# A new order for the end of a weight stream, another pitch for keys and values, and a last product written as four rows

## The chip, the cores and the metric

The kernel runs on one core of a Trainium2 chip. The metric is device time in microseconds (us), the median of several runs. A run's time is some 1.8 us above the span that the profile shows (370.68 against 368.9 in the profiled run of the kernel before); traces are told here in microseconds from the start of the span. The record has the span of every run, profiled or not. Every run told here was in the fast state.

The engines are called PE (matrix products), PEld (its weight loads), DVE (vector), ACT (activations), POOL and SP (which issues the large loads).

Ratios are the mean time of one kernel's fast runs over the mean of the other's fast runs of the same rounds, so they are not quite the ratio of the medians quoted beside them. Intervals are 95%.

## The reference

One token passes through a transformer block with adaptive layer norm. It attends with 32 query heads to 8 key/value heads of 32768 cached keys of 128 elements each, then goes through a small feed-forward layer. Cut to what matters:

```python
mod = (_silu(c) @ w_mod).reshape(c.shape[0], 6, 1, -1)       # sa, ca, ga, sb, cb, gb
h = _layernorm(x) * (1 + ca) + sa
q = h @ wq                                                   # 512 -> 32 heads x 128
o = softmax(q @ k_cache.T * Dh ** -0.5) @ v_cache            # 2 x 64 MB of keys and values
x = x + ga * (o @ wo)                                        # 4096 -> 512, 4 MB
h = _layernorm(x) * (1 + cb) + sb
x = x + gb * (relu(h @ w1) @ w2)                             # 512 -> 1792 -> 512, 1.8 + 1.8 MB
```

## The kernel before

All large inputs come through one queue of loads, issued in a fixed order into a ring of eight slots of 2 MB; a load is issued when the slot that it takes is free. Keys and values of one head group g come in four tiles (u = 0..3) of 2 MB, and the keys run one group ahead of the values.

```python
TK = 64
kv = A_k_cache[0].rearrange("g (u p j) d -> g u p j d", p=P, j=TK)   # one tile: 2 MB in one piece
vv = A_v_cache[0].rearrange("g (u p j) d -> g u p j d", p=P, j=TK)
w2_v = B_w2.rearrange("(p ft) d -> p ft d", p=P)
ring = ctx.enter_context(tc.tile_pool(name="ring", bufs=8))
ktpool = ctx.enter_context(tc.tile_pool(name="ktpool", bufs=4))
...
stream = [("wm", 0), ("wm", 1), ("wq", 0), ("wq", 1)]
stream += [("k", 0, u) for u in range(NTILE)]
for g in range(Hkv):
    for u in range(NTILE):
        if g + 1 < Hkv:
            stream.append(("k", g + 1, u))
        stream.append(("v", g, u))
    if g % GH == GH - 2:
        stream.append(("wo", g // GH))
stream += [("w1",), ("w2a",), ("w2b",)]
...
for g in range(Hkv):
    for u in range(NTILE):
        if g + 1 < Hkv:
            scores(g + 1, u)      # DVE transposes the keys, PE multiplies
        pv(g, u)                  # 16 products of 512 columns on PE
    if g + 1 < Hkv:
        softmax(g + 1)
    gather(g)
    if g % GH == GH - 1:
        project(g // GH)          # normalise, then 64 products with wo
```

So wo's second half is streamed between the values of group 6 and those of group 7, the last group. The tail computes in columns (512 values as 128 partitions x 4), and the output goes out as 128 pieces of four elements:

```python
w1_f = w1_sb[:].rearrange("p kt (m ft) -> p kt ft m", ft=FT)      # weights read with a step of 14
...
for part, base, n in (("w2a", 0, FT - W2B), ("w2b", FT - W2B, W2B)):
    for f in range(n):
        for ko in range(KT):
            nc.tensor.matmul(ffnT_ps[:, ko:ko + 1],               # 128 weights, one column
                lhsT=w2_sb[:, f, :].rearrange("p (m ko) -> p ko m", ko=KT)[:, ko, :],
                rhs=hidT[:, base + f:base + f + 1], ...)
...
nc.scalar.dma_start(out=out[0, 0].rearrange("(p kt) -> p kt", p=P), in_=outT_bf[:])
```

Of the kernel before, what the change touches and what calls it, by code (L numbers as in the profile page):

```python
# [9 lines left out]
BF16 = mybir.dt.bfloat16  # L10
# [7 lines left out]
def kernel(  # L18
# [29 lines left out]
    CH = P // HH  # L48
    RH = Dh // CH
    NHALF = Hkv // GH  # L50
    W2B = 2
    assert Dh == 128 and REP == 4 and D == 512 and Dff % P == 0 and NTILE == 4
    scale = float(Dh) ** -0.5
    eps = 1e-5


    kv = A_k_cache[0].rearrange("g (u p j) d -> g u p j d", p=P, j=TK)
    vv = A_v_cache[0].rearrange("g (u p j) d -> g u p j d", p=P, j=TK)
    wm_v = w_mod.rearrange("(p kt) n -> p kt n", p=P)
    wq_v = A_wq.rearrange("(p kt) n -> p kt n", p=P)  # L60
    wo_v = A_wo.rearrange("(b p r) d -> b p r d", p=P, r=RH)
    w1_v = B_w1.rearrange("(p kt) f -> p kt f", p=P)
    w2_v = B_w2.rearrange("(p ft) d -> p ft d", p=P)

    const = ctx.enter_context(tc.tile_pool(name="const", bufs=1))
    ring = ctx.enter_context(tc.tile_pool(name="ring", bufs=8))
    ktpool = ctx.enter_context(tc.tile_pool(name="ktpool", bufs=4))
    spool = ctx.enter_context(tc.tile_pool(name="spool", bufs=2))
    ps_s = ctx.enter_context(tc.tile_pool(name="ps_s", bufs=2, space=bass.MemoryType.PSUM))
    ps_o = ctx.enter_context(tc.tile_pool(name="ps_o", bufs=2, space=bass.MemoryType.PSUM))  # L70
# [9 lines left out]
    def load(key):  # L80
        kind = key[0]
        if kind == "wm":
            t = ring.tile([P, KT // 2, 6 * D], BF16, tag="slot", name="wm_sb")
            src = wm_v[:, 2 * key[1]:2 * key[1] + 2, :]
        elif kind == "wq":
            t = ring.tile([P, KT // 2, Hq * Dh], BF16, tag="slot", name="wq_sb")
            src = wq_v[:, 2 * key[1]:2 * key[1] + 2, :]
        elif kind == "k":
            t = ring.tile([P, TK, Dh], BF16, tag="slot", name="Ksb")
            src = kv[key[1], key[2]]  # L90
        elif kind == "v":
            t = ring.tile([P, TK, Dh], BF16, tag="slot", name="Vsb")
            src = vv[key[1], key[2]]
        elif kind == "wo":
            t = ring.tile([P, RH, D], BF16, tag="slot", name="wo_sb")
            src = wo_v[key[1]]
        elif kind == "w1":
            t = ring.tile([P, KT, Dff], BF16, tag="slot", name="w1_sb")
            src = w1_v
        elif kind == "w2a":  # L100
            t = ring.tile([P, FT - W2B, D], BF16, tag="slot", name="w2a_sb")
            src = w2_v[:, 0:FT - W2B, :]
        else:
            t = ring.tile([P, W2B, D], BF16, tag="slot", name="w2b_sb")
            src = w2_v[:, FT - W2B:FT, :]
        i = nc.sync.dma_start(out=t[:], in_=src)
        tc.stamp_issue_order_token(i.ins, "sp_stream")
        loaded[key] = t
# [3 lines left out]
    for g in range(Hkv):  # L112
        for u in range(NTILE):
            if g + 1 < Hkv:
                stream.append(("k", g + 1, u))
            stream.append(("v", g, u))
        if g % GH == GH - 2:
            stream.append(("wo", g // GH))
    stream += [("w1",), ("w2a",), ("w2b",)]
    pos = [0]  # L120

    def need(key):
        while key not in loaded:
            load(stream[pos[0]])
            pos[0] += 1
        return loaded[key]
# [106 lines left out]
                )  # L233
    modT_sb = const.tile([P, NMOD], F32)
    nc.vector.tensor_copy(out=modT_sb[:], in_=modT_ps[:])

    hT = const.tile([P, KT], BF16)
    layernorm_T(xT[:], hT[:], modT_sb[:, 0:KT], modT_sb[:, KT:2 * KT], "ln1")
# [128 lines left out]
                start=False, stop=(gl == GH - 1 and s == 3), skip_group_check=True,  # L367
            )

    def project(b):  # L370

        oh_ps = acc.pop(b)
        linv = spool.tile([HH, 1], F32, tag="linv", name="linv")
        nc.vector.reciprocal(out=linv[:], in_=oh_ps[:, Dh:Dh + 1])  # L374
        oh = spool.tile([HH, Dh], BF16, tag="oh_sb", name="oh_sb")
        nc.vector.tensor_scalar(
            out=oh[:], in0=oh_ps[:, 0:Dh], scalar1=linv[:], scalar2=None, op0=ALU.mult,
        )
        o2_ps = small_ps([P, RH], "o2_ps")
        for cc in range(CH):  # L380
            nc.tensor.matmul(  # L381
                o2_ps[:], lhsT=esel[:, cc, :, :].rearrange("h x y -> h (x y)"),
                rhs=oh[:, RH * cc:RH * (cc + 1)], start=(cc == 0), stop=(cc == CH - 1),
            )
        o2 = spool.tile([P, RH], BF16, tag="o2_sb", name="o2_sb")
        nc.vector.tensor_copy(out=o2[:], in_=o2_ps[:])
        wo_sb = need(("wo", b))
        for r in range(RH):
            for ko in range(KT):
                nc.tensor.matmul(  # L390
                    attnT_ps[:, ko:ko + 1],
                    lhsT=wo_sb[:, r, :].rearrange("p (m ko) -> p ko m", ko=KT)[:, ko, :],
                    rhs=o2[:, r:r + 1], start=False, stop=(b == NHALF - 1 and r == RH - 1),
                    skip_group_check=True,
                )
# [5 lines left out]
    for g in range(Hkv):  # L401
        if g + 1 < Hkv:
            build_qbd(g + 1)
        for u in range(NTILE):
            if g + 1 < Hkv:
                scores(g + 1, u)
            pv(g, u)
        PT_tiles.pop(g)
        if g + 1 < Hkv:
            softmax(g + 1)  # L410
        gather(g)
        if g % GH == GH - 1:
            project(g // GH)


    x1T = const.tile([P, KT], F32)
# [2 lines left out]
    h2T = const.tile([P, KT], BF16)  # L419
    layernorm_T(x1T[:], h2T[:], modT_sb[:, 3 * KT:4 * KT], modT_sb[:, 4 * KT:5 * KT], "ln2")  # L420

    w1_sb = need(("w1",))
    w1_f = w1_sb[:].rearrange("p kt (m ft) -> p kt ft m", ft=FT)
    hidT_ps = small_ps([P, FT], "hidT_ps")
    for ft in range(FT):
        for kt in range(KT):
            nc.tensor.matmul(  # L427
                hidT_ps[:, ft:ft + 1], lhsT=w1_f[:, kt, ft, :], rhs=h2T[:, kt:kt + 1],
                start=(kt == 0), stop=(kt == KT - 1),
            )  # L430
    hidT = const.tile([P, FT], BF16)
    nc.scalar.activation(out=hidT[:], in_=hidT_ps[:], func=ACT.Relu)
    ffnT_ps = small_ps([P, KT], "ffnT_ps")
    nc.vector.memset(ffnT_ps[:], 0.0)
    for part, base, n in (("w2a", 0, FT - W2B), ("w2b", FT - W2B, W2B)):
        w2_sb = need((part,))
        for f in range(n):
            for ko in range(KT):
                nc.tensor.matmul(  # L439
                    ffnT_ps[:, ko:ko + 1],  # L440
                    lhsT=w2_sb[:, f, :].rearrange("p (m ko) -> p ko m", ko=KT)[:, ko, :],
                    rhs=hidT[:, base + f:base + f + 1], start=False, stop=(base + f == FT - 1),
                    skip_group_check=True,
                )
    oT_f = const.tile([P, KT], F32)
    nc.vector.tensor_tensor(out=oT_f[:], in0=ffnT_ps[:], in1=modT_sb[:, 5 * KT:6 * KT], op=ALU.mult)
    outT_bf = const.tile([P, KT], BF16)
    nc.vector.tensor_tensor(out=outT_bf[:], in0=oT_f[:], in1=x1T[:], op=ALU.add)
    nc.scalar.dma_start(out=out[0, 0].rearrange("(p kt) -> p kt", p=P), in_=outT_bf[:])


# [28 lines left out]
```

## Time and profile before

| | before |
|---|---|
| time, median of 3 runs | 370.83 us (370.71 to 370.88) |
| span of the profiled execution | 368.9 us |
| bytes read, rate while the stream runs | 149.4 MB, 423 to 432 GB/s |
| last V tile landed | 346.84 us |
| first product with wo's second half | 353.44 us |
| output issued | 365.06 us |

From the page, the busy time of each engine (us, share of the span, instructions):

```profile
PE 287.7 (78%) x1616; PEld 124.1 (34%) x1616; DVE 179.2 (49%) x189; ACT 31.6 (9%) x73; POOL 9.4 (3%) x15
```

No compute engine is near 100%, while the transfers (shown in the prediction) are at one rate all the way to the tail. One more stretch of the timeline also belongs here later: the 64 products of the last group's V (start us, us, engine, line, operation, output and inputs, count, and in brackets the idle time before it and what ended it).

```profile
332.20 8.58 PE L353 MATMUL o_ps<-Vsb,PT_g 128*16 128x512 bf16 x32 [0.71 <-DMA Vsb<-in_A_v_cache_dram]
341.99 3.61 PE L353 MATMUL o_ps<-Vsb,PT_g 128*16 128x512 bf16 x16 [1.21 <-DMA Vsb<-in_A_v_cache_dram]
346.88 3.61 PE L353 MATMUL o_ps<-Vsb,PT_g 128*16 128x512 bf16 x16 [1.28 <-DMA Vsb<-in_A_v_cache_dram]
```

PE waits for each of the last tiles: it has caught up with the stream. The transfer of wo's second half, which comes just before these tiles, gave it the time. It even had time for a slow stretch: the first 32 products take 8.58 us, where two tiles at the pace of the last ones take 7.2, and PE still waits 1.21 us for the next tile. The granted clock (the share of full speed that PE is allowed) is low there; the last three values of a stretch are this clock, the DMA share and GB/s, after the busy time of PE, PEld, DVE, ACT and POOL:

```profile
330.00:335.00 5.00, 3.98 (x17) 1.74 (x18) 1.25 (x1) 0.27 (x2) 0.00 (x0) 0.69 0.99 423
```

Read in stretches of 0.5 us, it is 0.50 from 331.9 to 335.3 us.

### The profile page before, as it was taken

The numbers are of one execution on the slowest core, as the hardware profiler recorded it, in microseconds if no ns is written. First come the engines' busy times: TensorE is split into PE (matmuls) and PEld (weight loads), VectorE is DVE, ScalarE is ACT, GpSimd is POOL, SyncE is SP. The second block draws the span as 40 slices with busy tenths as digits, with TensorE's granted clock in tenths as the row PEclk, the third lists the DMA queues.
The fourth block names the chain that finished last, engine by engine and source line by source line (L and its number), as shares of the span: only waits on it lengthen the run. The fifth ranks groups of instructions, "written<-read, shape, count | busy, mean of one in ns | idle before, by whom it ended". The sixth has DMA issues, their size and how long they took to land.

```text
span 368.9 us, 3738 instructions
## 1 busy us (share of the span) xinstructions
PE 287.7 (78%) x1616; PEld 124.1 (34%) x1616; DVE 179.2 (49%) x189; ACT 31.6 (9%) x73; POOL 9.4 (3%) x15
## 2 busy tenths in 40 slices
PE   0448867987977798796878899987968799779755
PEld 0433322333322333232323343333323333233344
DVE  1419966556554464436454473546445645420020
ACT  1111031003000300012000300011000200020020
POOL 9000000000000000000000000000000000000000
PEclk9999998998999989986999979999989789998975
DMA  8999999999999999999999999999999999999920
GB/s 303 428 428 425 428 427 432 428 430 426 423 430 428 426 428 426 428 428 426 426 429 430 428 424 423 428 432 432 426 428 426 426 426 426 425 428 426 426 110 0
DMA packets 10960, 149.66 MB, mean 406 GB/s; under 512 B 1600, under 2 KB 1600, under 8 KB 1728
## 3 DMA queue, kind: packets, MB, share of 16 engines
q1 hardware_dynamic: 10512, 149.43, 95.6%
q8 instruction: 12, 0.20, 0.2%
q10 hardware_dynamic: 432, 0.00, 0.1%
q14 instruction: 4, 0.03, 0.0%
HBM read 149.42 MB, written 0.00 MB: 405 GB/s over the span
## 4 chain that ended last, share of the span: by engine, by line
DMA 75%; PE 11%; DVE 11%; ACT 1%; issue 1%; DVEq 0%
DMA Ksb<-in_A_k_cache_dram 64%; DVE KTt L287 10%; DMA Vsb<-in_A_v_cache_dram 9%; PE o_ps L353 4%; PE S_ps L296 4%; DMA xc_bf<-in_c_dram 2%; PE attnT_ps L390 1%; PE hidT_ps L427 1%; PE ffnT_ps L439 1%; PE oh_ps L365 0%; DVE S_g L302 0%; ACT P_g L329 0%; DVE PT_g L334 0%; ACT X L363 0%; PE o_ps L381 0%
## 5 line engine op out<-in xcount | busy, mean ns | idle before, releaser
L287 DVE STREAM_TRANSPOSE KTt<-Ksb 128x2048 f32<-128x2048 f32 x64 | 144.4, 2287 | 67.7 <-DMA Ksb<-in_A_k_cache_dram 67.7
L296 PE MATMUL S_ps<-KTt,qbd 128*128 128x512 bf16 x512 | 136.3, 416 | 34.3 <-DVE KTt L287 33.3
L353 PE MATMUL o_ps<-Vsb,PT_g 128*16 128x512 bf16 x512 | 119.7, 389 | 4.2 <-DMA Vsb<-in_A_v_cache_dram 3.2
L296 PEld LDWEIGHTS <-qbd 128*128 128x128 bf16 x512 | 51.4, 102 | 114.1 <-issue 70.2
L353 PEld LDWEIGHTS <-PT_g 128*16 128x16 bf16 x512 | 44.5, 91 | 77.0 <-issue 21.2
L302 DVE TENSOR_SCALAR_CACHE_REDUCE S_g<-S_ps 128x512 f32<-128x512 f32 x16 | 11.0, 688 | 38.7 <-PE S_ps L296 38.7
L266 ACT COPY qbd<-qrep_sb 32x128 bf16<-32x128 bf16 x32 | 9.4, 295 | 183.5 <-PE S_ps L296 182.4
L363 ACT COPY X<-o_ps 16x512 f32<-16x512 f32 x8 | 4.6, 574 | 106.3 <-PE o_ps L353 106.3
L334 DVE STREAM_TRANSPOSE PT_g<-P_g 128x1024 bf16<-128x1024 bf16 x8 | 9.7, 1218 | 7.4 <-ACT P_g L329 7.3
L230 PE MATMUL modT_ps<-siluT,wm_sb 128*128 128x1 bf16 x96 | 3.5, 172 | 12.4 <-DVE siluT L222 12.4
L314 DVE TENSOR_REDUCE Mrow<-mT_ps 1x4 f32<-1x128 f32 x8 | 2.2, 279 | 20.6 <-PE mT_ps L312 20.6
L365 PE MATMUL oh_ps<-X,osel 16*16 16x128 f32 x64 | 10.6, 313 | 1.1 <-ACT X L363 1.1
L340 PE MATMUL oh_ps<-l_g,lsel 128*16 128x1 f32 x16 | 1.6, 171 | 11.4 <-ACT P_g L329 11.4
L374 DVE RECIPROCAL linv<-oh_ps 16x1 f32<-16x1 f32 x2 | 0.3, 135 | 20.7 <-PE oh_ps L365 20.7
L329 ACT ACTIVATE P_g<-S_g,nbias 128x1024 bf16<-128x1024 f32 x8 | 9.2, 1148 | 0.4 <-ACT nbias L326 0.2
L244 PE MATMUL qT_ps<-hT,wq_sb 128*128 128x1 bf16 x128 | 3.7, 165 | 5.7 <-DMA wq_sb<-in_A_wq_dram 5.1
L230 PEld LDWEIGHTS <-wm_sb 128*128 128x128 bf16 x96 | 3.6, 119 | 12.3 <-DMA wm_sb<-in_w_mod_dram 7.1
L365 PEld LDWEIGHTS oh_ps<-X,osel 16*16 16x16 f32 x64 | 6.0, 103 | 3.5 <-ACT X L363 1.8
L324 PE MATMUL Mb_ps<-ident_f,Mexp 1*128 1x1 f32 x16 | 3.0, 256 | 3.7 <-DVE Mexp L319 3.7
L244 PEld LDWEIGHTS <-wq_sb 128*128 128x128 bf16 x128 | 3.6, 104 | 5.9 <-DMA wq_sb<-in_A_wq_dram 5.2
L340 PEld LDWEIGHTS oh_ps<-l_g,lsel 128*16 128x16 f32 x16 | 0.9, 97 | 12.6 <-ACT P_g L329 9.7
L427 PE MATMUL hidT_ps<-h2T,w_sb 128*128 128x1 bf16 x56 | 3.5, 198 | 1.7 <-DVE h2T L213 1.7
(79 smaller groups left out, 60.7 us busy)
## 6 DMA issues: line engine op xcount, KB each, us to landing
Ksb<-in_A_k_cache_dram SPq DMA_DIRECT2D x32, 2048.0 KB, 33.6
Vsb<-in_A_v_cache_dram SPq DMA_DIRECT2D x32, 2048.0 KB, 33.7
wq_sb<-in_A_wq_dram SPq DMA_DIRECT2D x2, 2048.0 KB, 17.1
wo_sb<-in_A_wo_dram SPq DMA_DIRECT2D x2, 2048.0 KB, 32.6
wm_sb<-in_w_mod_dram SPq DMA_DIRECT2D x2, 1536.0 KB, 8.1
w_sb<-in_B_w_dram SPq DMA_DIRECT2D x1, 1792.0 KB, 33.3
w2a_sb<-in_B_w_dram SPq DMA_DIRECT2D x1, 1536.0 KB, 32.7
w2b_sb<-in_B_w_dram SPq DMA_DIRECT2D x1, 256.0 KB, 27.9
```

Source lines behind the costliest of these rows:

```text
L230: nc.tensor.matmul(modT_ps[:, j * KT + ko:j * KT + ko + 1], lhsT=lhsT[:, ko, :], rhs=siluT[:, kt:kt + 1], start=(kt == 0), stop=(kt == KT ...
L244: nc.tensor.matmul(qT_ps[:, hq:hq + 1], lhsT=wq_sb[kt // 2][:, kt % 2, hq * Dh:(hq + 1) * Dh], rhs=hT[:, kt:kt + 1], start=(kt == 0), stop ...
L266: nc.scalar.copy(out=o, in_=i)
L287: nc.vector.transpose(out=KTt[:].bitcast(F32), in_=Ksb[:, 32 * half:32 * half + 32, :].rearrange("p j d -> p (j d)").bitcast(F32),)
L296: nc.tensor.matmul(S_ps[:], lhsT=qbd[g % 2][:, hp, s, :], rhs=KTv[:, 16 * sl:16 * sl + 16, h, :, par], start=(t4 == 0 and sl == 0 and hp = ...
L302: nc.vector.tensor_scalar(out=S_tiles[g][:, G, :], in0=S_ps[:], scalar1=1.0, scalar2=None, op0=ALU.mult, op1=ALU.max, accum_out=m_tiles[g] ...
L329: nc.scalar.activation(out=P_g[:], in_=S_g[:].rearrange("p g f -> p (g f)"), func=ACT.Exp, bias=nbias[:], scale=scale, accum_out=l_g[:],)
L334: nc.vector.transpose(out=PT_g[:], in_=P_g[:])
L353: nc.tensor.matmul(o_ps[:], lhsT=PT_g[:, c0:c0 + 16], rhs=Vsb[:].rearrange("p (s j) d -> p s j d", j=16)[:, :, j, :], start=(u == 0 and j ...
L363: nc.scalar.copy(out=X[:], in_=o_tiles.pop(g)[:])
L365: nc.tensor.matmul(acc[b][:, 0:Dh], lhsT=osel[:, gl, s, :], rhs=X[:, s * Dh:(s + 1) * Dh], start=False, stop=(gl == GH - 1 and s == 3), sk ...
L427: nc.tensor.matmul(hidT_ps[:, ft:ft + 1], lhsT=w1_f[:, kt, ft, :], rhs=h2T[:, kt:kt + 1], start=(kt == 0), stop=(kt == KT - 1),)
```

## The change

The intent is to shorten the tail. Both halves of wo move behind all values, so that the long chain from the last V tile (product, gather, normalise) runs while wo, w1 and w2 still stream. The rest is to make the tail itself cheaper. The core of the diff:

```diff
-    kv = A_k_cache[0].rearrange("g (u p j) d -> g u p j d", p=P, j=TK)
-    vv = A_v_cache[0].rearrange("g (u p j) d -> g u p j d", p=P, j=TK)
+    kv = A_k_cache[0].rearrange("g (p u j) d -> g u p j d", p=P, j=TK)
+    vv = A_v_cache[0].rearrange("g (p u j) d -> g u p j d", p=P, j=TK)
-    w2_v = B_w2.rearrange("(p ft) d -> p ft d", p=P)
+    w2_v = B_w2.rearrange("(a p b) d -> p a b d", p=P, b=FB)           # FB = 2
-    ktpool = ... bufs=4
+    ktpool = ... bufs=3
-        if g % GH == GH - 2:
-            stream.append(("wo", g // GH))
+    stream += [("wo", b) for b in range(NHALF)]
     stream += [("w1",), ("w2a",), ("w2b",)]
+    def rows4(src_T, name):                   # a column vector as four rows
+        r_ps = small_ps([P, P], f"{name}_ps")
+        nc.vector.memset(r_ps[:], 0.0)
+        for i in range(KT):
+            dst = r_ps[32 * i:32 * i + 1, :].rearrange("o (n kt) -> o kt n", kt=KT)
+            for kt in range(KT):
+                nc.tensor.matmul(dst[:, kt, :], lhsT=src_T[:, kt:kt + 1],
+                                 rhs=ident_f[:, 32 * i:32 * i + 32], start=True, stop=True, ...)
+        nc.vector.tensor_copy(out=r_sb[:], in_=r_ps[:])
+    gb_rows = rows4(modT_sb[:, 5 * KT:6 * KT], "gb_rows")
...
         if g % GH == GH - 1:
-            project(g // GH)
+            normalise(g // GH)
+    for b in range(NHALF):
+        project(b)
...
+    x1_rows = rows4(x1T[:], "x1_rows")
-    w1_f = w1_sb[:].rearrange("p kt (m ft) -> p kt ft m", ft=FT)
+    w1_f = w1_sb[:].rearrange("p kt (a m b) -> p kt a b m", m=P, b=FB)    # step of 2
...
+                for i in range(KT):                                        # four column tiles
+                    nc.tensor.matmul(ffn_ps[32 * i:32 * i + 1, :], lhsT=hidT[:, ft:ft + 1],
+                        rhs=w2_sb[:, a, b, i * P:(i + 1) * P], ...)
...
-    nc.scalar.dma_start(out=out[0, 0].rearrange("(p kt) -> p kt", p=P), in_=outT_bf[:])
+    nc.sync.dma_start(out=out[0, 0].rearrange("(i n) -> i n", i=KT),
+        in_=o_bf[:].rearrange("(i r) n -> i r n", r=32)[:, 0, :])
```

More of the change, by code (lines that the diff above doesn't have):

```diff
@@ L50 @@
     NHALF = Hkv // GH
-    W2B = 2
-    assert Dh == 128 and REP == 4 and D == 512 and Dff % P == 0 and NTILE == 4
+    FB = 2
+    FA = FT // FB
+    assert Dh == 128 and REP == 4 and D == 512 and Dff % (FB * P) == 0 and NTILE == 4
     scale = float(Dh) ** -0.5
     eps = 1e-5
-    kv = A_k_cache[0].rearrange("g (u p j) d -> g u p j d", p=P, j=TK)
-    vv = A_v_cache[0].rearrange("g (u p j) d -> g u p j d", p=P, j=TK)
+    kv = A_k_cache[0].rearrange("g (p u j) d -> g u p j d", p=P, j=TK)
+    vv = A_v_cache[0].rearrange("g (p u j) d -> g u p j d", p=P, j=TK)
     wm_v = w_mod.rearrange("(p kt) n -> p kt n", p=P)
@@ L62 @@
     w1_v = B_w1.rearrange("(p kt) f -> p kt f", p=P)
-    w2_v = B_w2.rearrange("(p ft) d -> p ft d", p=P)
+    w2_v = B_w2.rearrange("(a p b) d -> p a b d", p=P, b=FB)
     const = ctx.enter_context(tc.tile_pool(name="const", bufs=1))
     ring = ctx.enter_context(tc.tile_pool(name="ring", bufs=8))
-    ktpool = ctx.enter_context(tc.tile_pool(name="ktpool", bufs=4))
+    ktpool = ctx.enter_context(tc.tile_pool(name="ktpool", bufs=3))
     spool = ctx.enter_context(tc.tile_pool(name="spool", bufs=2))
@@ L100, in load @@
         elif kind == "w2a":
-            t = ring.tile([P, FT - W2B, D], BF16, tag="slot", name="w2a_sb")
-            src = w2_v[:, 0:FT - W2B, :]
-        else:
-            t = ring.tile([P, W2B, D], BF16, tag="slot", name="w2b_sb")
-            src = w2_v[:, FT - W2B:FT, :]
+            t = ring.tile([P, FA - 1, FB, D], BF16, tag="slot", name="w2a_sb")
+            src = w2_v[:, 0:FA - 1]
+        else:
+            t = ring.tile([P, 1, FB, D], BF16, tag="slot", name="w2b_sb")
+            src = w2_v[:, FA - 1:FA]
         i = nc.sync.dma_start(out=t[:], in_=src)
@@ L235 @@
     nc.vector.tensor_copy(out=modT_sb[:], in_=modT_ps[:])
+    def rows4(src_T, name):
[4 more added lines that the diff above has]
+            for kt in range(KT):
+                nc.tensor.matmul(
+                    dst[:, kt, :], lhsT=src_T[:, kt:kt + 1], rhs=ident_f[:, 32 * i:32 * i + 32],
+                    start=True, stop=True, skip_group_check=True,
+                )
+        r_sb = const.tile([P, P], F32, name=f"{name}_sb")
+        nc.vector.tensor_copy(out=r_sb[:], in_=r_ps[:])
+        return r_sb
+    gb_rows = rows4(modT_sb[:, 5 * KT:6 * KT], "gb_rows")
     hT = const.tile([P, KT], BF16)
@@ L368, in gather, with normalise @@
             )
-    def project(b):
+    o2_tiles = {}
+    def normalise(b):
         oh_ps = acc.pop(b)
@@ L386, in project @@
         nc.vector.tensor_copy(out=o2[:], in_=o2_ps[:])
+        o2_tiles[b] = o2
+    def project(b):
+        o2 = o2_tiles.pop(b)
         wo_sb = need(("wo", b))
@@ L427 @@
             nc.tensor.matmul(
-                hidT_ps[:, ft:ft + 1], lhsT=w1_f[:, kt, ft, :], rhs=h2T[:, kt:kt + 1],
+                hidT_ps[:, ft:ft + 1], lhsT=w1_f[:, kt, ft // FB, ft % FB, :], rhs=h2T[:, kt:kt + 1],
                 start=(kt == 0), stop=(kt == KT - 1),
@@ L432 @@
     nc.scalar.activation(out=hidT[:], in_=hidT_ps[:], func=ACT.Relu)
-    ffnT_ps = small_ps([P, KT], "ffnT_ps")
-    nc.vector.memset(ffnT_ps[:], 0.0)
-    for part, base, n in (("w2a", 0, FT - W2B), ("w2b", FT - W2B, W2B)):
+    ffn_ps = small_ps([P, P], "ffn_ps")
+    nc.vector.memset(ffn_ps[:], 0.0)
+    for part, base, n in (("w2a", 0, FA - 1), ("w2b", FA - 1, 1)):
         w2_sb = need((part,))
-        for f in range(n):
-            for ko in range(KT):
-                nc.tensor.matmul(
-                    ffnT_ps[:, ko:ko + 1],
-                    lhsT=w2_sb[:, f, :].rearrange("p (m ko) -> p ko m", ko=KT)[:, ko, :],
-                    rhs=hidT[:, base + f:base + f + 1], start=False, stop=(base + f == FT - 1),
-                    skip_group_check=True,
-                )
-    oT_f = const.tile([P, KT], F32)
-    nc.vector.tensor_tensor(out=oT_f[:], in0=ffnT_ps[:], in1=modT_sb[:, 5 * KT:6 * KT], op=ALU.mult)
-    outT_bf = const.tile([P, KT], BF16)
-    nc.vector.tensor_tensor(out=outT_bf[:], in0=oT_f[:], in1=x1T[:], op=ALU.add)
-    nc.scalar.dma_start(out=out[0, 0].rearrange("(p kt) -> p kt", p=P), in_=outT_bf[:])
+        for a in range(n):
+            for b in range(FB):
+                ft = (base + a) * FB + b
+                for i in range(KT):
+                    nc.tensor.matmul(
+                        ffn_ps[32 * i:32 * i + 1, :], lhsT=hidT[:, ft:ft + 1],
+                        rhs=w2_sb[:, a, b, i * P:(i + 1) * P], start=False, stop=(ft == FT - 1),
+                        skip_group_check=True,
+                    )
+    o_rows = const.tile([P, P], F32)
+    nc.vector.tensor_tensor(out=o_rows[:], in0=ffn_ps[:], in1=gb_rows[:], op=ALU.mult)
+    o_bf = const.tile([P, P], BF16)
+    nc.vector.tensor_tensor(out=o_bf[:], in0=o_rows[:], in1=x1_rows[:], op=ALU.add)
+    nc.sync.dma_start(
+        out=out[0, 0].rearrange("(i n) -> i n", i=KT),
+        in_=o_bf[:].rearrange("(i r) n -> i r n", r=32)[:, 0, :],
+    )
 _INS = ['A_x', 'A_k_cache', 'A_v_cache', 'A_wq', 'A_wo', 'B_x', 'B_w1', 'B_w2', 'c', 'w_mod']
```

## The prediction

> **What bounds the kernel now.** I read the page's slices first, then the transfer issues, the chain of waits, the stretches of the last 25 us, and the timeline of the tail.
>
> The slices (40 slices of 9.22 us; tenths busy, then GB/s):
>
> ```profile
> DMA  8999999999999999999999999999999999999920
> GB/s 303 428 428 425 428 427 432 428 430 426 423 430 428 426 428 426 428 428 426 426 429 430 428 424 423 428 432 432 426 428 426 426 426 426 425 428 426 426 110 0
> ```
>
> The 16 DMA engines never starve: 423 to 432 GB/s for some 345 us, then nothing. So the span has two parts: a stream of 149.4 MB whose rate is set by the engines, and a tail in which nothing moves. Compute is not the bound in the first part (PE is busy 78% and DVE 49% of the span). Work taken from the middle is worth nothing; the time changes only through the rate of the stream or through the tail.
>
> The tail, from the chain that ended last (start us, us, what):
>
> ```profile
> 312.30 34.54 DMA Vsb<-in_A_v_cache_dram
> 346.84 0.04 issue
> 346.88 3.63 PE o_ps L353 x16
> ...
> 353.44 2.27 PE attnT_ps L390 x64
> 355.74 0.17 DVE x1T L417
> ...
> 358.89 3.48 PE hidT_ps L427 x56
> 362.40 0.19 ACT hidT L432
> 362.59 0.04 issue
> 362.63 2.01 PE ffnT_ps L439 x56
> 364.67 0.17 DVE oT_f L446
> 364.86 0.16 DVE outT_bf L448
> ```
>
> The last V tile lands at 346.84, and everything after it is serial: its product, the gather and normalisation up to 353.44, the wo product, layer norm, w1, w2, output. Only w1, w2a and w2b (3.58 MB) stream meanwhile. From the issue lines, start plus time to landing puts them at 317.80 + 33.3 = 351.1, 322.11 + 32.7 = 354.8 and 327.62 + 27.9 = 355.5 us: each has landed before the chain wants it (358.9, 362.6 and 364.2). Thus the end follows from the landing of the last V tile, 22 us before it.
>
> The output transfer and the stretch behind (issue line: times to landing, last column):
>
> ```profile
> wo_sb<-in_A_wo_dram SPq DMA_DIRECT2D x2, 2048.0 KB, 32.6
> out_dram<-outT_bf ACTq DMA_DIRECT2D x1, 1.0 KB, 2.8
> ```
>
> It is issued at 365.06, lands at 367.86, and the span ends 1.04 us later at 368.9. The timed median is 370.83.
>
> [...] The keys and values go from a 16 KB pitch (one contiguous 2 MB block per tile) to 64 KB[...]. The trace has one case between: wq's tiles are 16 KB pieces 32 KB apart, and they land within the stretch from 12 to 22 us, which ran at 431 GB/s against 427 for 27 to 346 us. [...] No four-tile product is in this trace. [...] granted clock 1.00 up to 355 us, 0.50 from 356 on.
>
> **The change part by part.**
>
> *Stream order.* Both wo tiles (2 MB each) move behind all V. Total bytes and the 3.58 MB at the end stay, so wo's second half takes exactly the place of the last V tile: if the rate holds, it lands at 346.84. The last V tile lands 2 x 4.9 = 9.8 us earlier, near 337.0; with its product, gather and normalisation (346.84 to 353.44, 6.6 us) it is done by 343.6, the first wo product (2.3 us) by 345.9, all under the wo stream. The instruction order agrees: both normalisations and the first 64 wo products precede the second's wait. So the chain starts with a 2.27 us product at 346.9 rather than with the V product: saved 353.44 - 346.88 = 6.56 us.
>
> *Rows for the residual.* x1 is turned into four rows by 16 fp32 products of 1 x 32, listed between the statistics product and w1 on PE. On DVE the copy of their result stands ahead of the layer norm's reciprocal in program order[...], so the layer norm must wait for them. Each fp32 product is two instructions in this trace; eight with 128 columns took 1.06 us at full clock (0.13 each). With 32 columns at half clock I take 0.055 each: 32 x 0.055 = 1.75 us, plus some 0.25 for the result and 0.3 for the copy of 128x128. The reciprocal came 357.95 - 356.56 = 1.39 us after the start of the statistics product; now it comes 0.58 + 1.75 + 0.25 + 0.3 = 2.9 us after. Cost: 1.5 us. The same 16 products for the gate run at 16 us, under the stream, where wq's second half was awaited until 22.1: free.
>
> *w1 product.* Its weights were read with a step of 14 elements; 56 products took 3.48 us, 62 ns each. The wo and w2 products, with a step of 4, took 2.27/64 = 35 and 2.01/56 = 36 ns, the latter at half clock. The new split of w1 makes the step 2. I take 34 ns: 1.9 us. Saved: 1.55 us.
>
> *w2 product.* 56 products, now a one-column weight with 128 moving columns, in four column tiles. The last V tile's 16 products of 512 columns took 3.63 us at full clock, 0.227 each, so 128 columns take 57 ns, or some 113 at half clock. If four run side by side that is 28 ns each; issue at some 36 ns, as above, is the floor. I take 2.3 us for 2.01. Cost: 0.3 us.
>
> *End.* Two DVE operations on 128x128 instead of 128x4: 0.16 us each becomes about 0.24 (a cast of 128x128 from PSUM took 0.29). Cost: 0.15 us. The output goes as four pieces of 256 B rather than 128 of 8 B; I guess 2.3 us for 2.8. Saved: 0.5 us.
>
> *Sum.* -6.56 + 1.5 - 1.55 + 0.3 + 0.15 - 0.5 = -6.65 us. Check against the stream: the w2 product then starts at about 356.1, after w2a (354.8, perhaps 0.3 later for its 2 KB pieces where it had 12 KB) and w2b (about 355.8). They are near but do not bind. 370.83 - 6.65 = 364.2 us.
>
> *The rest.* Three transposed-key buffers for four: a K and V pair costs PE (136.3 + 119.7)/32 = 8.0 us and DVE 4.5, within the 9.8 us in which it arrives; issues run 34 us ahead of landing, so short stalls do not reach the stream.
>
> **The rivals.** *The pitch slows the stream*: 134 of 149 MB are K and V. [...] the wq stretch speaks against it. *The pitch helps*: the rate runs down unevenly, which says that the 16 engines do not finish together:
>
> ```profile
> core 0: us, PE busy (x) PEld busy (x) DVE busy (x) ACT busy (x) POOL busy (x), PEclk, DMA share, GB/s
> ...
> 350.00:351.00 1.00, 0.49 (x3) 0.00 (x0) 0.00 (x0) 0.47 (x1) 0.00 (x0) 1.00 0.94 399
> 351.00:352.00 1.00, 0.84 (x8) 0.66 (x8) 0.00 (x0) 0.98 (x2) 0.00 (x0) 1.00 0.89 367
> 352.00:353.00 1.00, 0.37 (x9) 0.18 (x8) 0.49 (x2) 0.41 (x1) 0.00 (x0) 1.00 0.59 244
> 353.00:354.00 1.00, 0.74 (x26) 0.75 (x23) 0.17 (x1) 0.00 (x0) 0.00 (x0) 1.00 0.32 129
> ```
>
> The shortfall against 427 from 350 to 355.5 us adds up to some 1150 GB/s times us, or 2.7 us of streaming: were all engines even, every late landing would come up to 2.7 us sooner, for 361.5. Nothing in the trace ties the skew to the addresses of K and V. *The column tiles do not overlap*: 56 x 113 ns = 6.3 us, 4 more than assumed: 368. *The rows cost nothing or double*: between 362.7 and 366. *w2b becomes the bound*: this needs a chain 0.5 us faster than mine, and then caps the gain: 355.8 + 0.3 + 0.6 + 2.3 + 1.0 gives a span of 360, or 362 timed.
>
> **Range and chances.** The terms of the tail are good to about 1.5 us together, and the stream adds a tail on each side: I give 65% to an unchanged rate, 20% to a faster one and 15% to a slower one. That makes 361.0 to 368.0. The 2% line is at 363.4, only 0.8 us under the sum, so faster by over 2% gets 0.36, within 2% 0.60, and slower by over 2% (over 378.2) 0.04.
>
> **What would show it right or wrong.** Right: the chain's last transfer is wo and lands near 346.8; the wo product follows at once; layer norm takes about 4.6 us from x1 to h2 instead of 3.1; w1's 56 products take under 2.2 us. Wrong: GB/s slices other than 423 to 432 (the pitch); the last wo landing elsewhere; 56 w2 products over 4 us (no overlap of tiles); a w2 product that waits for w2b; V products not finished when wo lands.

## The result, and the profile after

The changed kernel took 362.59 us (median of 4 runs, 361.87 to 363.16), the kernel before 370.86 in the same rounds: ratio 0.9776, interval 0.9755 to 0.9797. It is faster by 2.2%, inside the predicted range of 361.0 to 368.0, but 1.6 us below the predicted 364.2 and on the other side of the 2% line from the likeliest class.

The profiled execution was the quickest of the four (361.87 us, span 360.1). Its slices:

```profile
DMA  8999999999999999999999999999999999999992
GB/s 302 428 430 430 431 423 426 428 431 426 426 431 428 428 424 431 428 426 430 428 427 428 431 421 428 431 424 428 431 430 424 426 435 420 430 431 428 424 404 92
```

The stream runs at the same rate as before; the idle end has shrunk from more than one slice to less than one (a slice is now 9.0 us). The chain that ended last, from 322 us on:

```profile
322.49 32.39 DMA w2a_sb<-in_B_w_dram
354.88 0.14 issue
355.01 1.69 PE ffn_ps L469 x56
356.70 0.02 issue
356.73 0.30 DVE o_rows L475
```

From there on the chain passes through none of the last group's V tiles, wo or w1. Its last wait is for w2a, which lands at 354.88, where it landed before (354.8). The tail in the timeline:

```profile
326.46 14.02 PE L371 MATMUL o_ps<-Vsb,PT_g 128*16 128x512 bf16 x64
...
343.10 2.29 PE L414 MATMUL attnT_ps<-o_sb,wo_sb 128*128 128x1 bf16 x64
346.75 2.29 PE L414 MATMUL attnT_ps<-o_sb,wo_sb 128*128 128x1 bf16 x64 [1.36 <-DMA wo_sb<-in_A_wo_dram]
349.08 0.16 DVE L443 TENSOR_TENSOR x1T<-attnT_ps,modT_sb 128x4 f32<-128x4 f32 x1 [5.70 <-PE attnT_ps L414]
...
350.42 1.16 PE L245 MATMUL x_rows_ps<-ident_f,x1T 128*1 128x32 f32 x32
...
351.61 0.29 DVE L250 COPY x_rows_sb<-x_rows_ps 128x128 f32<-128x128 f32 x1 [0.67 <-PE x_rows_ps L245]
...
352.75 1.63 PE L455 MATMUL hidT_ps<-h2T,w_sb 128*128 128x1 bf16 x56 [1.17 <-DVE h2T L214]
...
355.01 1.45 PE L469 MATMUL ffn_ps<-w2a_sb,hidT 128*1 128x128 bf16 x48 [0.63 <-DMA w2a_sb<-in_B_w_dram]
```

Wo's second half lands where the last V tile had landed, and its product follows at once, 6.7 us sooner than before. The 64 V products of the last group now run without a pause: with wo gone from between groups 6 and 7, PE has no spare time there. The last V tile was issued at 305.71 and landed 31.1 us later, at 336.8; PE came to its 16 products at 337.0.

The difference of the two spans, step by step, from the two timelines:

| step | before | after | moved by | predicted |
|---|---|---|---|---|
| start of the product with wo's second half | 353.44 | 346.75 | -6.69 | -6.56 |
| x1 to the w1 product | 355.74 to 358.89 | 349.08 to 352.75 | +0.52 | +1.5 |
| w1 product to its relu | 358.89 to 362.40 | 352.75 to 354.42 | -1.84 | -1.55 |
| relu to the w2 product | 362.40 to 362.63 | 354.42 to 355.01 | +0.36 | 0 |
| w2 product to the gate on DVE | 362.63 to 364.67 | 355.01 to 356.73 | -0.32 | +0.3 |
| two operations on DVE | 364.67 to 365.06 | 356.73 to 357.37 | +0.25 | +0.15 |
| output issue to the end | 365.06 to 368.9 | 357.37 to 360.1 | -1.11 | -0.5 |
| sum | | | -8.83 | -6.66 |

The spans differ by 368.9 - 360.1 = 8.8 us. (The prediction writes its sum as -6.65; its terms add to -6.66.) The table explains the quick execution, not yet the others: the median run is 0.7 us slower than this one.

### The profile page after: what moved, and what is told of

Same layout as the page of the kernel before. It is cut to its first block, busy times and chain, and to the rows that moved or that the text cites. A ratio compares the mean times of both kernels' runs of the same rounds, so it can differ in the third digit from the quotient of the medians.

```text
span 360.1 us, 3889 instructions
## 1 busy us (share of the span) xinstructions
PE 283.2 (79%) x1680; PEld 123.2 (34%) x1680; DVE 180.3 (50%) x193; ACT 31.6 (9%) x73; POOL 9.4 (3%) x15
## 4 chain that ended last, share of the span: by engine, by line
DMA 86%; DVE 6%; issue 5%; PE 2%; DVEq 0%
DMA Ksb<-in_A_k_cache_dram 76%; DMA w2a_sb<-in_B_w_dram 9%; DVE KTt L305 6%; DMA xc_bf<-in_c_dram 2%; PE o_ps L371 1%; PE S_ps L314 1%; PE ffn_ps L469 0%; DVE S_g L320 0%; DVE o_rows L475 0%; DVE o_bf L477 0%; DVEq L305 0%; PE mT_ps L330 0%
## 5 line engine op out<-in xcount | busy, mean ns | idle before, releaser
L314 PE MATMUL S_ps<-KTt,qbd 128*128 128x512 bf16 x512 | 133.7, 411 | 34.4 <-DVE KTt L305 33.5
L371 PE MATMUL o_ps<-Vsb,PT_g 128*16 128x512 bf16 x512 | 117.9, 385 | 1.1 <-DVE PT_g L352 1.0
L414 PE MATMUL attnT_ps<-o_sb,wo_sb 128*128 128x1 bf16 x128 | 4.6, 172 | 1.4 <-DMA wo_sb<-in_A_wo_dram 1.4
## 6 DMA issues: line engine op xcount, KB each, us to landing
w2a_sb<-in_B_w_dram SPq DMA_DIRECT2D x1, 1536.0 KB, 32.4
```

The costliest lines, as they stand in the source:

```text
L314: nc.tensor.matmul(S_ps[:], lhsT=qbd[g % 2][:, hp, s, :], rhs=KTv[:, 16 * sl:16 * sl + 16, h, :, par], start=(t4 == 0 and sl == 0 and hp = ...
L371: nc.tensor.matmul(o_ps[:], lhsT=PT_g[:, c0:c0 + 16], rhs=Vsb[:].rearrange("p (s j) d -> p s j d", j=16)[:, :, j, :], start=(u == 0 and j ...
L414: nc.tensor.matmul(attnT_ps[:, ko:ko + 1], lhsT=wo_sb[:, r, :].rearrange("p (m ko) -> p ko m", ko=KT)[:, ko, :], rhs=o2[:, r:r + 1], start ...
```

## The experiments

All ran on chips with the kernel before beside them. The changed kernel is the base of each, unless said otherwise.

| kernel | median us (lowest to highest) | ratio to before | interval |
|---|---|---|---|
| changed kernel, first time | 362.59 (361.87 to 363.16) | 0.9776 | 0.9755 to 0.9797 |
| after_again | 363.03 (362.20 to 363.33) | 0.9784 | 0.9771 to 0.9798 |
| keys16 | 362.02 (361.92 to 362.62) | 0.9764 | 0.9751 to 0.9777 |
| before64_kt3 | 370.82 (370.55 to 371.45) | 0.9998 | 0.9990 to 1.0006 |
| order_only | 365.83 (364.49 to 366.47) | 0.9862 | 0.9843 to 0.9881 |
| order_warm | 364.88 (364.25 to 365.47) | 0.9838 | 0.9825 to 0.9852 |
| warm | 362.14 (362.12 to 362.18) | 0.9765 | 0.9751 to 0.9778 |
| act_out | 362.57 (362.06 to 363.49) | 0.9778 | 0.9764 to 0.9793 |
| w1step | 363.77 (363.71 to 366.35) | 0.9816 | 0.9800 to 0.9831 |
| one_tile | 367.54 (367.00 to 368.58) | 0.9913 | 0.9899 to 0.9928 |
| rows_act | 362.11 (361.92 to 362.45) | 0.9762 | 0.9749 to 0.9776 |
| act_split | 361.39 (361.11 to 362.34) | 0.9749 | 0.9735 to 0.9763 |
| warm_split | 361.36 (361.23 to 361.45) | 0.9744 | 0.9731 to 0.9757 |

### The base again

after_again is the changed kernel without an edit.

> The changed kernel once more, beside the others on the same chip, as the base for their small differences. All theories: 362.0 to 363.2 us, ratio near 0.978. In the tail the wo product of the second half starts near 346.8, layer norm takes 3.7 us from x1 to the w1 product, and the w2 product waits some 0.4 us for w2a.

It came in at 363.03 us. Its profiled execution (span 361.4) was a different one, and it showed the thing that the first profile hid:

```profile
327.48 16.23 PE L371 MATMUL o_ps<-Vsb,PT_g 128*16 128x512 bf16 x64
...
346.32 0.82 PE L414 MATMUL attnT_ps<-o_sb,wo_sb 128*128 128x1 bf16 x20
```

The 64 V products start 1.0 us later than in the first profile and take 2.2 us longer. So the first wo product starts at 346.32 instead of 343.10, when wo's second half has nearly landed, and both halves (4.4 us) run back to back behind it: x1 is reached at 350.79 instead of 349.08. The wait of the w2 product for w2a, expected here too, was gone. The stretches say what is different, first after_again, then the first profile (us, busy PE, PEld, DVE, ACT, POOL with counts, granted PE clock, DMA share, GB/s):

```profile
325.00:330.00 5.00, 4.48 (x17) 1.91 (x18) 1.25 (x1) 0.47 (x2) 0.00 (x0) 0.52 1.02 433
330.00:335.00 5.00, 5.00 (x20) 1.94 (x19) 0.00 (x0) 0.00 (x0) 0.00 (x0) 0.79 1.01 429
...
325.00:330.00 5.00, 4.71 (x27) 2.29 (x28) 1.25 (x1) 0.13 (x2) 0.00 (x0) 1.00 1.02 436
330.00:335.00 5.00, 5.00 (x25) 2.08 (x24) 0.00 (x0) 0.00 (x0) 0.00 (x0) 1.00 1.01 429
```

The granted clock is 0.52 and 0.79 where it was 1.00 in the first profile. In stretches of 0.5 us the clock of after_again is 0.50 from 325.2 to 332.1 us, that of act_out from 327.5 to 330.9. Read in the same way, every such spell before the tail lasts some 3.41 or 6.82 us in the first profile (8 spells) and in the kernel before (11), and within one trace the changes lie whole multiples of some 3.41 us apart (first profile: 279.96, 286.79, 293.62 and 344.82 us, so 2, 2 and 15 of them). Where they fall against the work differs from trace to trace. Nor is PE simply idle ahead of this one: before the V products it has small products to do, from 322.8 to 327.5 us here, its longest gap is 1.5 us, and in the 3.4 us before the drop it was busy for 1.54 us. What sets a spell off is not shown, and how little work it takes to prevent one, no run here tests.

### The pitch, and the third buffer

keys16 puts keys and values back to one piece per tile:

```diff
-    kv = A_k_cache[0].rearrange("g (p u j) d -> g u p j d", p=P, j=TK)
+    kv = A_k_cache[0].rearrange("g (u p j) d -> g u p j d", p=P, j=TK)     # vv likewise
```

> The changed kernel with keys and values back at a 16 KB pitch, all else kept. Theory (the pitch is neutral; the gain is all in the tail): within 0.4 us of the changed kernel, GB/s slices of 423 to 435, wo's second half lands within 0.5 us of 346.8. Rival (the pitch is part of the gain): slower by 1 us or more, wo's second half landing that much later. Other rival (the pitch costs something): faster by 1 us or more.

It took 362.02 us, 1.0 below after_again, which touches the line of the other rival, and 0.6 below the first runs; the intervals overlap. W1 landed at 316.80 + 34.1 = 350.9 us, as in the changed kernel (316.98 + 34.0 = 351.0). The stream does not see the pitch: its full slices run from 420 to 434 GB/s here and from 420 to 435 in the changed kernel. By the times alone the verdict is less clean, because the base itself scatters.

before64_kt3 therefore puts the two parts alone into the kernel before, whose times scatter little:

```diff
+    kv = A_k_cache[0].rearrange("g (p u j) d -> g u p j d", p=P, j=TK)     # vv likewise
-    ktpool = ... bufs=4
+    ktpool = ... bufs=3
```

> The kernel before with two parts of the change alone: keys and values 64 KB apart per partition, and three buffers of transposed keys instead of four; stream order, tail and output as before. Theory (neither moves the stream): 370.6 to 371.2 us, slices of 423 to 432 GB/s, w1 landing within 0.3 us of 351.1. Rival (the pitch or the missing buffer costs something that the shorter tail hid, or the pitch helps): a difference of 1 us or more.

The ratio is 0.9998, interval 0.9990 to 1.0006: no change is seen, within 0.1%. W1 landed at 317.57 + 33.5 = 351.1 us. (No run has four buffers in the changed kernel.)

### The order alone

order_only is the kernel before with the stream's order changed and the normalisation split from the wo product, those parts of the diff above and no others.

> The kernel before with the stream order alone changed: wo behind all V, normalisation split from the wo product; pitch, w1 and w2 layouts, three products and output as before. Theory: the tail starts with the wo product near 346.8 instead of with the V product, 6.6 us sooner, and nothing else moves: 364.2 us (ratio 0.982), w1's product waits up to 0.3 us for nothing or for w1, which landed at 351.1. Rival (the order only moves a wait, because w1 or w2 land too late or PE is late with V): over 365.5 us, with a transfer of w1 or w2 in the chain.

It took 365.83 us, above the line that the rival named, and ranged over nearly 2 us. But no transfer of w1 or w2 stood in the chain. In its profiled execution (365.81 us) the V products took 15.67 us from 327.51, the two wo products ran back to back from 345.81, and x1 came at 350.44. PE was late with V, as in after_again; the rival had named that too, beside a late transfer. In this trace the clock was also at 0.50 from 314.6 to 318.1 us, where PE multiplies the last keys.

### Keeping PE busy before the last V products

warm adds eight products into a PSUM tile that nobody reads, between the last group's softmax sums and its V products:

```diff
         nc.scalar.mul(out=nbias[:], in_=Mb_ps[:], mul=-scale)
+        if g == Hkv - 1:
+            nc.gpsimd.tensor_copy(out=wl[:], in_=<nbias, repeated 128 times>)   # ties them to this moment
+            w_ps = ps_s.tile([P, 512], F32, tag="s", name="w_ps")
+            for i in range(8):
+                nc.tensor.matmul(w_ps[:], lhsT=wl[:], rhs=<512 columns of qbd[0]>,
+                                 start=(i == 0), stop=(i == 7))
```

> The changed kernel plus eight products of 512 columns whose result nobody reads, put on PE into its idle time between the last group's softmax sums and the last group's 64 V products (some 324.2 to 326.5 us). Theory: with wo moved away, the last group's V products follow its softmax at once, on a PE that has just been idle; where the clock drops there, the 64 products take 15.7 to 16.3 us instead of 14.0, the first wo product comes at 345 to 346 us instead of 343.1, and both wo products then stand in the chain. With PE kept busy the 64 products take 14.0 to 14.5 us, the second wo product waits for its transfer again, and the times gather at the fast end: 361.6 to 362.3 us, spread under 0.8. Rival (the clock drops whatever PE does there, or the spread has another cause): 362 to 363.4 as before. Other rival: the eight products delay V by more than they help.

The four runs lie within 0.06 us: 362.12 to 362.18. The trace:

```profile
325.00:330.00 5.00, 5.00 (x29) 2.32 (x28) 1.25 (x1) 0.49 (x2) 0.00 (x0) 1.00 1.02 433
330.00:335.00 5.00, 5.00 (x25) 2.10 (x24) 0.00 (x0) 0.00 (x0) 0.00 (x0) 1.00 1.02 429
...
327.56 13.98 PE L383 MATMUL o_ps<-Vsb,PT_g 128*16 128x512 bf16 x64
...
344.16 2.29 PE L426 MATMUL attnT_ps<-o_sb,wo_sb 128*128 128x1 bf16 x64
347.01 2.29 PE L426 MATMUL attnT_ps<-o_sb,wo_sb 128*128 128x1 bf16 x64 [0.56 <-DMA wo_sb<-in_A_wo_dram]
```

The V products start 1.1 us later than in the quick execution, because the eight stand before them. But they run at full pace and clock, and the second wo product waits for its transfer again. The expected 361.6 to 362.3 us held, and so did the spread. The other traces fit the same reading:

| profiled run | clock at 0.50, 310 to 340 us | V products from | take us | first wo product | x1 at | timed us |
|---|---|---|---|---|---|---|
| changed kernel | - | 326.46 | 14.02 | 343.10 | 349.08 | 361.87 |
| act_split | - | 326.60 | 14.01 | 343.23 | 349.12 | 361.11 |
| warm | - | 327.56 | 13.98 | 344.16 | 349.33 | 362.13 |
| warm_split | - | 327.28 | 13.98 | 343.88 | 349.08 | 361.23 |
| order_warm | - | 327.47 | 13.98 | 344.09 | 349.30 | 365.19 |
| act_out | 327.5 to 330.9 | 326.74 | 15.67 | 345.05 | 349.51 | 362.18 |
| one_tile | 328.0 to 331.4 | 326.76 | 15.67 | 345.05 | 349.51 | 367.78 |
| keys16 | 324.6 to 331.4 | 326.96 | 16.14 | 345.72 | 350.18 | 362.62 |
| after_again | 325.2 to 332.1 | 327.48 | 16.23 | 346.32 | 350.79 | 363.33 |
| order_only | 314.6 to 318.1, 328.3 to 331.7 | 327.51 | 15.67 | 345.81 | 350.44 | 365.81 |
| rows_act | 314.9 to 318.3, 328.5 to 331.9 | 327.74 | 15.67 | 346.05 | 350.51 | 362.45 |
| w1step | 316.2 to 319.7, 326.5 to 333.3 | 328.51 | 16.33 | 347.49 | 351.95 | 366.35 |

(order_only and order_warm have the tail of the kernel before behind x1.) An earlier spell, from 314 to 320 us, slows the last score products instead: from first to last they then take 5.3 us rather than 4.1, and V starts that much later. The eight products come after it; no run tests a remedy for it.

x1 comes 2.3 us after wo's second half lands or some 4.5 us after the first wo product starts, whichever is later. So the V products may end about 1.5 us later than in the quick execution before x1 moves (343.10 + 1.5 + 4.5 = 349.1), and the wait for w2a takes up another 0.4 before the end does.

order_warm is order_only with the same eight products.

> The kernel before with the stream order alone changed, plus the eight products. Without them it took 364.49 to 366.47 us, where the prediction's term for the order alone says 364.2 to 364.3. Theory (the miss of some 1.5 us is the slow V products): 364.2 to 364.8 us. Rival (the order itself is worth less than 6.6 us): 365.5 or more.

It took 364.88 us (364.25 to 365.47): 1.0 us less than order_only, 0.6 more than the term says, between the two theories' lines though within 0.1 us of the first. In the trace the order alone does what was said: V products in 13.98 us, the wo product at 346.96, x1 at 349.30 rather than 355.74 (6.4 us sooner), span 362.4, which is 6.5 below the span of before. That run was timed at 365.19, so 2.8 us above its span where others are 1.8. The record settles where the extra microsecond is: the spans of all four runs are 362.3 to 362.6 us, against 368.9 to 369.4 for the kernel before in the same rounds, so the order is worth 6.6 us in each of them, as the theory says. The times lie 1.8 to 3.2 us above these spans; the extra is outside the span, and what it is stays open.

### The output

act_out issues the four rows from ACT's queue:

```diff
-    nc.sync.dma_start(
+    nc.scalar.dma_start(
         out=out[0, 0].rearrange("(i n) -> i n", i=KT), ...
```

> The changed kernel with the output issued from the ACT queue, as before the change, still as four rows. From the issue to the span's end it took 3.84 us before (128 pieces of 8 B, ACT) and 2.73 after (4 pieces of 256 B, SP). Theory (fewer pieces save it): 2.6 to 2.9 us again, same time within 0.3 us. Rival (the SP queue saves it): 3.5 us or more, the kernel 0.8 us slower. Side expectation: the issue itself was 0.35 us on ACT and 0.66 on SP, so ACT might save 0.3 us.

From the issue at 357.55 to the end at 360.3 it took 2.75 us, against 2.73 from SP, and the time is the same (362.57). So the form of the transfer (four pieces for 128) counts, not the queue. one_tile, below, adds a third point: one piece of 1 KB took 366.0 - 363.77 = 2.2 us. The other traces with 128 pieces took 3.8 to 4.2 us. The side expectation was wrong: the issue on ACT took 1.09 us, not 0.35.

### The step of w1

w1step goes back to a step of 14 elements for w1, with w2 split to match; rows and tiles stay:

```diff
-    w2_v = B_w2.rearrange("(a p b) d -> p a b d", p=P, b=FB)
+    w2_v = B_w2.rearrange("(p a b) d -> p a b d", p=P, b=FB)
-    w1_f = w1_sb[:].rearrange("p kt (a m b) -> p kt a b m", m=P, b=FB)
+    w1_f = w1_sb[:].rearrange("p kt (m a b) -> p kt a b m", m=P, b=FB)
```

> The changed kernel with w1 and w2 split as before the change, so that w1's weights are read with a step of 14 elements again and w2 in pieces of 12 KB per partition; rows and tiles kept. Theory (the step sets the pace of the 56 products): 3.5 us instead of 1.7 for w1's products (62 ns each); as the w2 product then no longer waits for w2a (0.4 us), the kernel is 1.4 us slower. Rival (the step doesn't matter, the faster product came from elsewhere): 1.7 us, no difference. Also: w2a lands within 0.3 us of where it does in the changed kernel if the 2 KB pieces cost nothing.

```profile
355.62 3.46 PE L455 MATMUL hidT_ps<-h2T,w_sb 128*128 128x1 bf16 x56 [1.17 <-DVE h2T L214]
```

3.46 us for 56 products, as before the change, instead of 1.63. The ratio is 0.9816 against 0.9776 and 0.9784 for the base, so 0.4% of 371 or some 1.3 us, near the 1.4 expected (the run that was profiled, 366.35, also had the slowest V products of all). W2a landed at 323.86 + 30.9 = 354.8 us with 12 KB pieces and at 322.49 + 32.4 = 354.9 with 2 KB pieces: the small pieces cost nothing that shows.

### The four tiles

one_tile writes all w2 products (and the rows) to partition 0, as one row of 512:

```diff
-    ffn_ps = small_ps([P, P], "ffn_ps")
+    ffn_ps = small_ps([1, KT, P], "ffn_ps")
-                        ffn_ps[32 * i:32 * i + 1, :], lhsT=hidT[:, ft:ft + 1],
+                        ffn_ps[:, i, :], lhsT=hidT[:, ft:ft + 1],
```

> The changed kernel with the w2 product and the rows in one column tile: all 56 products go to one partition with 512 columns, the output as one row. Theory (the four tiles run side by side): without them the 56 products of 128 columns at half clock take 56 x 0.107 to 0.113 = 6.0 to 6.3 us instead of 1.7. The rows' products, which were four in a row in one tile already, stay near 1.2 us, or slow if they overlapped. DVE on 1x512 takes some 0.6 us per operation instead of 0.3 (a copy of 16x512 took 0.57 on ACT), three of them in the path: 0.9 us more. In all 5 us slower, 367.8. Rival (issue sets the pace, not the tiles): 56 products in 1.7 to 2.0 us, the kernel 1 us slower.

In the chain of waits:

```profile
356.24 6.09 PE ffn_ps L469 x56
```

6.09 us where four tiles took 1.69: 109 ns per product against 30, a factor of 3.6. The whole took 367.54 us against an expected 367.8. The rows slowed as well, from 1.16 to 1.87 us. So it seems that even they, issued four in a row to the same tile, had gained from the tiles.

### The layer norm behind the rows

rows_act has ACT copy the x1 rows, so that DVE is free for the layer norm:

```diff
-    x1_rows = rows4(x1T[:], "x1_rows")
+    x1_rows = rows4(x1T[:], "x1_rows", nc.scalar.copy)     # copy engine as an argument
```

> The changed kernel with the copy of the x1 rows moved from DVE to ACT, behind the square root, so that the layer norm on DVE doesn't stand behind it. Theory (the stream is now the bound: the w2 product waits for w2a): the w1 product starts about 0.5 us sooner, the wait for w2a grows from 0.4 to some 0.9 us, the time stays within 0.3 us of the changed kernel. Rival (the chain of products is the bound): 0.5 us faster.

362.11 us: 0.5 us below the base's first runs and 0.9 below after_again, with an interval that overlaps both. That is nearer the rival (0.5) than the theory (within 0.3). In the profiled execution the V products were slow (15.67 us), w2's product did not wait for w2a, and x1 to the w1 product took 353.67 - 350.51 = 3.16 us, as before the change, instead of 3.67. There the chain of products is the bound and the half microsecond counts. In a quick execution the wait for w2a should eat it; none was profiled, but the fastest run, 361.92 us, is no faster than the base's (361.87), which fits. So each theory seems to hold in one kind of execution.

act_split adds a third piece of w2:

```diff
-    stream += [("w1",), ("w2a",), ("w2b",)]
+    stream += [("w1",), ("w2a",), ("w2m",), ("w2b",)]      # 768, 768 and 256 KB
```

> The same, and w2 loaded in three pieces (768, 768 and 256 KB) rather than two (1536 and 256). Theory (the end of the stream bounds): the w2 product starts when its first piece is there, before the second lands, and only the last products wait for the last pieces; w2's products end 0.4 to 0.9 us sooner than in the changed kernel, time 361.7 to 362.2. Rival: the later pieces land later for being more transfers, and nothing is won.

```profile
354.18 0.81 PE L470 MATMUL ffn_ps<-w2a_sb,hidT 128*1 128x128 bf16 x24 [0.27 <-ACT hidT L461]
354.94 0.81 PE L470 MATMUL ffn_ps<-w2m_sb,hidT 128*1 128x128 bf16 x24
355.58 0.38 PE L470 MATMUL ffn_ps<-w2b_sb,hidT 128*1 128x128 bf16 x8
```

The first products run before the second piece is there, and the last end at 356.0 rather than at 356.7. The time is 361.39 us, a little better than the range given (361.7 to 362.2).

warm_split is act_split with the eight products of warm.

> The same eight products in the version with the x1 copy on ACT and w2 in three pieces. Theory: 361.0 to 361.5 us in every run, below both kernels; without the products that version took 361.11 to 362.34. Rival: no difference.

361.36 us, all five runs within 0.22 us. The median is that of act_split; only the scatter is gone, so the medians alone would have shown no difference. It beats both kernels, the changed one by 0.3 to 0.4% (the interval is clear of after_again's and just meets that of the first runs).

## Why the prediction was right or wrong

**The bound and the stream: right.** The end of the stream stays where it was (w2a at 354.9 us after, 354.8 before), and pitch and third buffer are worth nothing (0.9998). Three slices (420, 421 and 435 GB/s) leave the range of 423 to 432 that was to show an effect of the pitch, but slices of keys16 with the old pitch do so too, and the mean of slices 2 to 37 is 427.9 after and 427.3 before. (The 3.58 MB of loads behind the last V tile are 3584 KB, so 3.67 MB; nothing rests on it.) The 15% for a slower stream and the 20% for a faster one, the author's estimates, were not needed.

**The stream order: right where PE keeps up, and incomplete.** -6.69 us in the quick execution, -6.4 in order_warm, against -6.56. The step that failed is the sentence that the V product, gather, normalisation and first wo product would all be done by 345.9, "all under the wo stream". It took the last V product from its landing, as if PE were waiting for it. In the kernel before that was so only because wo's second half gave PE a pause before the last group, long enough to swallow a spell at half clock (331.9 to 335.3 us). In the quick execution it held with nothing to spare: the tile landed at 336.8, PE came to it at 337.0, and the first wo product was done at 345.4. The prediction had not worked out when PE would come to that tile, so that agreement is luck. Without the pause the 64 products follow their softmax in one go, on a PE that may be at half clock (0.50). In seven of the nine executions tabled above without the eight products they took 15.7 us or more, and the first wo product came up to 4.4 us later than in the quick one, 1.2 us of it through the score products in three of them. The spells were in sight: the prediction reads the granted clock as "1.00 up to 355 us", but its own stretch from 312 to 340 us showed 0.94. Its list names "V products not finished when wo lands" as a sign of being wrong, but gave it no term in the sum; nor is it quite what happened, for in after_again they end at 343.7 and wo's second half lands at about 346.9. Late was the first wo product, which then ran into the second. Keeping PE busy removes this (warm): with the eight products all three traces show full clock there (1.00 from 315 to 340 us), and the spans of the 13 runs lie within 0.4 us for each kernel.

**The rows: mechanism right, size off.** The copy does hold up the reciprocal (in the first profile the square root on ACT ends at 351.26 us, the copy starts at 351.61 and the reciprocal at 351.82; with the copy on ACT, in rows_act, the reciprocal at 352.73 follows the square root's end at 352.71), but the 32 instructions took 1.16 us (36 ns each), not 1.75 (55 ns). The layer norm grew by 0.52 us, not 1.5. The 55 ns had been scaled from products of 128 columns that all went to one tile; in one_tile the same 32 took 1.87 us, which is 58 ns. So what was left out was that the tiles help here too.

**w1: right, a little more.** -1.84 for -1.55; 29 ns per product, not 34. w1step confirms the step as the cause.

**w2: overlap right, floor wrong.** Four tiles do run side by side (56 products in 1.69 us, against 6.09 in one_tile). The assumed 2.3 us stood on a floor of 36 ns per product for the issue, but it is 30 ns with a one-column weight: 1.69 us. The 36 ns came from products whose weights are read with a step of 4; at a step of 2 they took 29, so 36 was no floor of the issue. The rival without overlap is what one_tile measured, 6.1 us against the 6.3 said.

**Output: direction right, size off.** -1.11 for -0.5; the guess was for the landing, and a small number of pieces saves more than that. On DVE +0.25 for +0.15.

**The rival "w2b becomes the bound": partly so.** The tail came out faster than summed, and in quick executions the w2 product then waits 0.4 us, for w2a rather than w2b, so the chain's last transfer is w2a, where the list of signs had wo. The room was named (a chain faster by 0.5 us) but not counted.

In all, the terms that were too cautious make 1.0 + 0.3 + 0.6 + 0.6 = 2.5 us, less 0.4 for w2a and 0.1 for DVE; with 0.1 for the order that makes the 2.2 us between the table's sums. The median run lies 0.7 us above the quick one, which leaves about the measured 1.6; in the executions that were profiled it is the slow V products, in some the slow score products before them, that make this difference. The prediction said that the 2% line lay only 0.8 us below its number, and gave that side 0.36.

## What to carry to other kernels

When a transfer is moved out of the middle of a stream, ask who was using the pause that it made: the engine behind it may have been just fast enough with it, and without it a dip of the clock reaches the end (here a clock of 0.50 from 325.2 to 332.1 us, and 64 products in 16.2 us instead of 14.0). A tail is read term by term from the timeline, and each term wants a duration of the same kind of instruction (same step of the weights, same tiles, same number of pieces of a transfer). Where a kernel's times scatter and the kernel before does not, profile it twice before explaining a difference of half a per cent.

## Figures from these runs

- The granted clock: 0.50 in spells of some 3.41 or 6.82 us before the tail (11 in the kernel before, 8 in the first profile of the changed one). In after_again the longest gap was 1.5 us and PE was busy for 1.54 of the 3.41 us before the drop, and yet a block of 64 products went from 14.0 to 16.2 us. Eight products whose result nobody reads ended that (runs within 0.06 us instead of 1.3).
- The step of the weights, per product with one moving column: step 2, 29 ns (w1 in the changed kernel); step 4, 36 ns (w2 in the kernel before); step 14, 62 ns (w1 in the kernel before, and again in w1step). In the traces of the two kernels the granted clock was 0.50 in all three. What makes the step cost this, no run here tests.
- Four column tiles with a one-column weight and 128 moving columns: 3.6x (30 against 109 ns in one_tile). The idle time before the first of them, after the relu, was 0.27 us in act_split, as it was before the first w2 product of the kernel before, which has no such tiles.
- A pitch of 64 KB with 16 KB pieces costs nothing that shows: 0.9998 (0.9990 to 1.0006) in before64_kt3.
- The output, from its issue to the end of the span: 128 pieces of 8 B, 3.84 us (kernel before); 4 of 256 B, 2.73 (changed kernel); 1 of 1 KB, 2.2 (one_tile); for the four pieces it made no difference which of the two queues issued them (2.73 and 2.75).
